# A fused attention, MoE and top-2 MoE kernel: GpSimd drains inside the expert loop, and the overflow count loaded earlier

## The chip, the cores and the metric

The kernel runs as one program on one core of a Trainium2 chip. Five engines work side by side and meet only at semaphores: TensorE (PE in the rows; its weight loads are PEld), VectorE (DVE), ScalarE (ACT), GpSimd (POOL) and SyncE (SP). Each has a sequencer that takes its instructions in order; what the sequencer itself executes (waits, branches, register loads, drains) has a q behind the engine's name in the rows, as POOLq. The metric is device time in microseconds (us), the median of several runs.

## The reference, cut to what matters

The inputs are 4 batches of 576 tokens (2304 in all) with 512 features, 8 heads, 8 experts with 1024 hidden units.

```
x   = window attention over q, k, v                  # each token sees 64 positions
x   = relu(x @ w_in)**2 @ w_out                      # first MoE block: one dense MLP, 512 -> 2048 -> 512
lg  = x @ w_gate + log1p(exp(x @ w_noise)) * noise   # 8 noisy logits a token
top2, weights = two largest logits and their softmax
for e in range(8):                                   # second MoE
    for k in range(2):
        rows = top2[:, k] == e
        out[rows] += weight * (relu(x[rows] @ w1[e]) @ w2[e])
```

## The kernel before, in words

The program has four stretches. Attention for 2304 tokens and the dense MLP are interleaved, in six groups of 384 tokens. Gating runs along with it and writes a table: for each of 8 experts 624 slots (CAP, five tiles of up to 128), and in each slot a token and its weight. The second MoE then goes through the experts in nine passes (the loop at L709): passes 0 and 1 are the two halves of expert 0, passes 2 to 8 are experts 1 to 7. Behind the last pass stands a loop for tokens that found no slot (L782). Its trip count comes from the data, and here it is zero: the engines branch past it.

GpSimd has three kinds of work in the second MoE:

- `prep` gathers the rows of the next pass's tokens from DRAM into SBUF, five indirect DMAs of 128 rows a pass (L546, tiles `gx`). TensorE transposes them.
- `split` (L147) makes two parts of each expert weight tile: ScalarE writes the first, and GpSimd the second as a difference (L149, tile `w`), 16 for each expert. They are made for the expert that comes next, so TensorE needs them a pass later.
- `finish` (L587) gathers what earlier experts added to the output rows (`gy`, L546), VectorE computes `y` (L594), and the sums are scattered back (L552). The gathers must wait until the scatters of the expert before have landed, since they read the same tensor.

A scheduler of the framework orders the instructions of each engine: an instruction is placed when the data that it needs should be there. Instructions stay in the order of the text only where a dependence or a pin says so.

The number of overflow tiles is computed on VectorE with 14 small operations (L769 to L777). The scheduler puts them right behind the last gating, early in the second MoE. `values_load` (L780) then has every engine's sequencer load that number from SBUF into a register, with one instruction that the rows call TENSOR_LOAD. SyncE's stands early; those of the other four stand behind their last work, just ahead of the branch of the loop.

When the loop is skipped, GpSimd sets forward the semaphores that the loop's own indirect DMAs would have set (INC_SWDGE_SEM, L782), all engines go through a row of waits (L782), and the program ends (L872): each engine drains, that is, its sequencer waits until its engine has nothing left, and they meet at a barrier; GpSimd clears semaphores, and they meet again.

Of the kernel before, what the change touches and what calls it, by code (L numbers as in the profile page):

```python
# [8 lines left out]
F32 = mybir.dt.float32  # L9
F32R = mybir.dt.float32r  # L10
BF = mybir.dt.bfloat16
I32 = mybir.dt.int32
U32 = mybir.dt.uint32
AF = mybir.ActivationFunctionType
OP = mybir.AluOpType
# [25 lines left out]
def moe_kernel(ctx, tc, q, k, v, w_in, w_out, wg, wn, noise, w1, w2, out):  # L41
    nc = tc.nc
    B, H, S, D = q.shape
    N, DM = out.shape
    E, _, F2 = w1.shape
# [13 lines left out]
    CAP = 624  # L59
# [2 lines left out]
    FAR = 65536.0  # L62
    NEG = -1e30

# [1 line left out]
    consts = ctx.enter_context(tc.tile_pool(name="consts", bufs=1))  # L66
    hw = ctx.enter_context(tc.tile_pool(name="hw", bufs=2))
    xtp = ctx.enter_context(tc.tile_pool(name="xtp", bufs=2))
# [13 lines left out]
    def ps(tag):  # L82
        return psum.tile([128, 512], F32, name=tag, tag=tag, bufs={"o": 3, "h": 2, "att": 3}[tag])

# [1 line left out]
    warm = consts.tile([128, 128], BF, name="warm")  # L86
    nc.vector.memset(warm, 0.0)
    ident = consts.tile([128, 128], F32, name="ident")
# [27 lines left out]
    base = consts.tile([128, E], F32, name="base")  # L116
# [26 lines left out]
        nc.vector.tensor_copy(noi.rearrange("p t e -> p e t"),  # L143
                              pn[:, :N // 128 * E].rearrange("p (e t) -> p e t", e=E))

# [1 line left out]
    def split(dst, src):  # L147
        nc.scalar.activation(dst[:, 0], src, AF.Copy)  # L148
        nc.gpsimd.tensor_sub(dst[:, 1], src, dst[:, 0].bitcast(F32))  # L149
# [41 lines left out]
        for x in worder[len(wres):n]:  # L191
            wres[divmod(x, 2)] = moe1_half(*divmod(x, 2))

# [1 line left out]
    late = {}  # L195

    def att_loads(b, s, h0, nh, pool):
# [122 lines left out]
                    load_v(g * UG + i + 2)  # L320
                yield

# [1 line left out]
    L1out, outs, x2s = {}, {}, {}  # L324

    def products(p, n, w, x, cs=range(NCC)):
# [48 lines left out]
                nc.sync.dma_start(x2d[TG * g + 128 * t:TG * g + 128 * t + 128, :], x2)  # L375
                x2s[g].append(x2)

# [1 line left out]
    GAT = {}  # L379

    def gating(g):
# [125 lines left out]
    nc.gpsimd.iota(tok, pattern=[[128, N // 128], [0, 2]], base=1, channel_multiplier=1,  # L507
                   allow_small_or_imprecise_dtypes=True)

# [1 line left out]
    slot = {}  # L511

    def index_tables(lo, hi):
        n = hi - lo
        code = table[:, lo:hi, 0]
        V = nc.vector
        f = consts.tile([128, 2, n], F32, name=f"ixf{lo}")
        ix = consts.tile([128, n], I32, name=f"ix{lo}")
        w = consts.tile([128, n], F32, name=f"wt{lo}")
        V.tensor_add(w, table[:, lo:hi, 1], table[:, lo:hi, 2])  # L520
        # a slot that nobody took points beyond the last row, each to another one
        V.tensor_scalar(f[:, 0], code, 0.0, None, op0=OP.is_equal)
        V.tensor_scalar(f[:, 1], f[:, 0], FAR, pidx, op0=OP.mult, op1=OP.add)
        V.tensor_mul(f[:, 1], f[:, 1], f[:, 0])
        V.scalar_tensor_tensor(f[:, 1], f[:, 1], -1.0, code, op0=OP.add, op1=OP.add)
        V.tensor_copy(ix, f[:, 1])
        for j in range(n):
            slot[lo + j] = (ix[:, j:j + 1], w[:, j:j + 1])
# [16 lines left out]
    def gather(dst, src, i):  # L545
        nc.gpsimd.indirect_dma_start(  # L546
            out=dst, out_offset=None, in_=src[:, :],
            in_offset=bass.IndirectOffsetOnAxis(ap=slot[i][0][:dst.shape[0]], axis=0),
            bounds_check=N - 1, oob_is_err=False)

    def scatter(src, i):
        return nc.gpsimd.indirect_dma_start(  # L552
            out=out[:, :], out_offset=bass.IndirectOffsetOnAxis(ap=slot[i][0][:src.shape[0]], axis=0),
            in_=src, in_offset=None, bounds_check=N - 1, oob_is_err=False)
# [18 lines left out]
    def m2_L1(e, f, n, xT):  # L573
        if n <= 512:
            parts = ((0, n),)
        else:
            parts = ((0, n // 2), (n // 2, n // 2))
        h = M2["h"].tile([128, 2, n], F32R, name="h")
        for a, m in parts:
            ph = ps("h")  # L580
            products(ph, m, w2s[e, f][0], xT[:, :, :, a:a + m])
            nc.scalar.activation(h[:, 0, a:a + m], ph[:, :m], AF.Relu)  # L582
            nc.vector.scalar_tensor_tensor(h[:, 1, a:a + m], ph[:, :m], 0.0, h[:, 0, a:a + m].bitcast(F32),  # L583
                                           op0=OP.max, op1=OP.subtract)
        return h

    def finish(e, tiles, o):  # L587
        ys, sc = [], []
        for j, i in enumerate(tiles):
            if e > 0:  # L590
                m = min(128, CAP - 128 * j)
                y = hp2.tile([128, DM], F32, name="y", bufs=CT)[:m]
                gather(gy[j][:m], out, i)
                nc.vector.scalar_tensor_tensor(y, o[j][:m], slot[i][1][:m], gy[j][:m], op0=OP.mult, op1=OP.add)  # L594
            else:
                y = hw.tile([128, DM], F32, name="x2", bufs=3)
                nc.scalar.activation(y, o[j], AF.Copy, scale=slot[i][1])
            ys.append(y)
        for j, i in enumerate(tiles):
            st = scatter(ys[j], i)  # L600
            for x in sc:
                tc.declare_no_dep(st.ins, x.ins, reason="an expert's slots hold different rows")
            sc.append(st)

# [1 line left out]
    fill = []  # L606
    left = [0]

# [4 lines left out]
    def filler(n):  # L613
        while n > 0 and fill:
            gen = fill.pop(0)
            try:
                next(gen)
                n -= 1
                left[0] -= 1
                fill.append(gen)  # L620
            except StopIteration:
                pass
# [13 lines left out]
    for h0 in range(0, H, HL):  # L636
        for s in range(TG // SB):
            ld, parts = att_loads(0, s, h0, HL, att0)
# [23 lines left out]
    for g in range(NG):  # L662
# [42 lines left out]
    passes = [(0, list(range(TT))), (0, list(range(TT, CT)))] + [  # L705
        (e, list(range(CT * e, CT * e + CT))) for e in range(1, E)]
    xcur = xA
    gy = []
    for n, (e, tiles) in enumerate(passes):  # L709
        T = 128 * len(tiles) if e == 0 else CAP  # L710
        if n == 1:
            GAT["pool"].release()
            ringb.release()
            hp2 = tc.alloc_tile_pool(name="hp2", bufs=2)
            M2["stg"].release()
            stg3 = tc.alloc_tile_pool(name="stg3", bufs=4)
            M2["x"] = xp2 = tc.alloc_tile_pool(name="xp2", bufs=2, side="right")
        if n == 2:
            M2["h"] = hp2
        if n == 1:  # L720
            M2["stg"] = stg3
        pending = []
        o = None
        hprev = None
        for f in range(NF2 + 1):
            if f < NF2:
                h = m2_L1(e, f, T, xcur)
            filler(1)
            if f == (P0F if n == 0 else PNF) and n == 0:
                drain()  # L730
                index_tables(TT, NS)
            pending += [(hprev, w2s[e, f - 1][1])] if f else []
            if pending and not (n + 1 == len(passes) and f == NF2 - 1):
                if o is None:
                    o = [ps("o" if j < 3 else "att") for j in range(len(tiles))]
                accumulate(o, pending, f == 1, f == NF2)
                pending = []
                filler(1)
            hprev = h
            # next expert's weights  # L740
            if n >= 1 and f < NF2 and e + 1 < E:
                w2s[e + 1, f] = stage2(e + 1, f)
            if f == (P0F if n == 0 else PNF) and n + 1 < len(passes):
                nt = passes[n + 1][1]
                if n == 0:
                    xnext = xtp.tile([128, 2, NCC, 256], F32R, name="xT")
                else:
                    xnext = M2["x"].tile([128, 2, NCC, 128 * CT], F32R, name="x2T2")
                add_fill(prep(nt, xnext), len(nt))
        drain()  # L750
        if e > 0 and not gy:
            for j in range(CT):
                t = hp2.tile([128, DM], F32, name=f"gy{j}", bufs=1)
                nc.vector.memset(t, 0.0)
                gy.append(t)
        finish(e, tiles, o)
        if n + 1 < len(passes):
            xcur = xnext
# [1 line left out]
    V = nc.vector  # L760
    M2["x"].release()
    gxp.release()
    stg3.release()
    hp2.release()
    ovp = tc.alloc_tile_pool(name="ovp", bufs=1)
    nt = consts.tile([128, E], F32, name="nt")
    ni = consts.tile([128, E], I32, name="ni")
    te = consts.tile([128, E + 1], F32, name="te")
    V.tensor_scalar(nt, base, float(CAP), 0.0, op0=OP.subtract, op1=OP.max)  # L769
    V.tensor_scalar(nt, nt, 127.0, None, op0=OP.add)  # L770
    V.tensor_copy(ni, nt)
    V.tensor_scalar(ni, ni, 7, None, op0=OP.logical_shift_right)
    V.tensor_copy(nt, ni)
    V.memset(te[:, :1], 0.0)
    for e in range(E):
        V.tensor_add(te[:, e + 1:e + 2], te[:, e:e + 1], nt[:, e:e + 1])
    V.tensor_copy(ni[:, :1], te[:, E:])  # L777
    it = consts.tile([128, 1], F32, name="it")
    V.memset(it, 0.0)
    n_more = nc.values_load(ni[0:1, 0:1], min_val=0, max_val=2 * N // 128)  # L780
    NT2 = 2 * N // 128
    with tc.For_i(0, n_more):  # L782
        ee, pp, ww = (info[:, c].rearrange("p t j -> p (t j)") for c in range(3))
        tt = tok.rearrange("p t j -> p (t j)")
        oh = ovp.tile([128, NT2, E], F32, name="oh2")
# [90 lines left out]
```

## Time and profile before

| | us |
|---|---|
| median of 3 runs | 1067.27 (1066.27 to 1068.43) |
| span of the profiled execution, first to last instruction | 1071.7 |
| TensorE busy in it | 1020.3 |
| GpSimd busy in it | 410.5 |

The profiled execution has its span as its own time; it lies 4.4 us above the median of the runs that were not profiled. In the rows below, "busy" counts an engine's own work and leaves out what its sequencer does. A view by source line lists the sequencer's instructions too, and those are what the end of this kernel consists of.

### The profile page before, as it was taken

How to read it: one execution, taken by the hardware profiler on the slowest of the kernel's cores; microseconds unless marked ns; L12 is line 12 of the kernel's file. 1: busy time of each engine (PE TensorE's matmuls, PEld its weight loads, DVE VectorE, ACT ScalarE, POOL GpSimd, SP SyncE). 2: the span in 40 equal slices, each digit the busy share in tenths (PEclk: the TensorE clock that was granted, in tenths of full speed). 3: DMA queues.
4: the chain of work that ended last, by engine and by line, in shares of the span. 5: the costliest groups of instructions: out<-in, count | busy, mean ns of one | idle time of the engine just before them, and what ended most of it. 6: DMA issues, size and time to landing. Idle time of an engine off the chain costs nothing. (4 is left out here: it accounts for less than half of the span.)

```text
span 1071.7 us, 16784 instructions
## 1 busy us (share of the span) xinstructions
PE 1020.3 (95%) x6120; PEld 902.0 (84%) x6120; DVE 509.4 (48%) x1195; ACT 418.0 (39%) x1037; POOL 410.5 (38%) x405
## 2 busy tenths in 40 slices
PE   8877899999999999999899989999999999999994
PEld 6655788888888888888789879889988989998883
DVE  7999967437635744744854612131313122222311
ACT  4655555335434444543433235333323333323210
POOL 3565632001100210200450077666665657573501
PEclk9999899999999999999999989999999999999997
DMA  9655546112112112102320245443444445351201
GB/s 197 176 169 154 152 131 211 39 36 71 35 35 76 34 29 75 39 20 60 109 70 33 77 131 180 149 136 123 144 143 124 145 124 165 103 157 57 91 1 46
DMA packets 148736, 108.33 MB, mean 101 GB/s; under 512 B 85753, under 2 KB 126713, under 8 KB 148651
## 3 DMA queue, kind: packets, MB, share of 16 engines
q1 hardware_dynamic: 139451, 80.09, 26.2%
q0 software_dynamic: 9200, 27.14, 8.1%
q8 instruction: 50, 0.82, 0.3%
q14 instruction: 35, 0.29, 0.1%
HBM read 89.27 MB, written 20.48 MB: 102 GB/s over the span
## 5 line engine op out<-in xcount | busy, mean ns | idle before, releaser
L346 PE MATMUL o<-w,h 128*128 128x512 f32 x1488 | 393.0, 402 | 20.7 <-DVE h L359 12.5
L346 PEld LDWEIGHTS o<-w,h 128*128 128x128 f32 x1488 | 270.9, 189 | 78.7 <-DVE h L359 15.8
L329 PE MATMUL h<-xT,w 128*128 128x384 f32 (+1 forms) x1344 | 263.8, 344 | 3.2 <-DVE xT L287 1.9
L329 PEld LDWEIGHTS h<-xT,w 128*128 128x128 f32 x1344 | 231.5, 192 | 8.7 <-POOL w L149 2.4
L149 POOL TENSOR_TENSOR w<-st,w 128x512 fp32r<-128x512 f32 x128 | 165.3, 1299 | 102.6 <-ACT w L148 82.8
L329 PE MATMUL h<-x2T,w 128*128 128x312 f32 x1344 | 201.4, 306 | 0.0
L329 PEld LDWEIGHTS h<-x2T,w 128*128 128x128 f32 x1344 | 195.8, 188 | 3.6
L583 DVE SCALAR_TENSOR_TENSOR h<-h 128x312 fp32r<-128x312 f32 (+2 forms) x128 | 61.9, 484 | 278.9 <-ACT h L582 263.1
L148 ACT ACTIVATE w<-st 128x512 fp32r<-128x512 f32 x128 | 80.7, 631 | 193.3 <-PE att L346 119.7
L268 POOL TENSOR_TENSOR P<-P,stat 128x384 f32<-128x384 f32 x48 | 41.8, 872 | 219.2 <-DVE stat L267 103.7
L356 ACT ACTIVATE r<-h 128x384 f32<-128x384 f32 x96 | 46.7, 487 | 142.2 <-PE h L329 124.2
L582 ACT ACTIVATE h<-h 128x312 fp32r<-128x312 f32 (+2 forms) x128 | 54.5, 425 | 120.1 <-PE h L329 115.0
L346 PE MATMUL att<-w,h 128*128 128x512 f32 (+1 forms) x336 | 94.3, 393 | 0.0
L358 DVE TENSOR_TENSOR r<-r 128x384 f32<-128x384 f32 x80 | 53.9, 673 | 69.8 <-ACT h L357 68.5
L346 PEld LDWEIGHTS att<-w,h 128*128 128x128 f32 (+1 forms) x336 | 61.0, 181 | 15.4
L359 DVE TENSOR_TENSOR h<-r,h 128x384 fp32r<-128x384 f32 x96 | 60.6, 631 | 4.9 <-POOL r L358 2.2
L546 POOL DMA_INDIRECT gx<-x2d,ix x40 | 40.9, 1023 | 50.5 <-PE att L564 41.3
L552 POOL DMA_INDIRECT out_dram<-y,ix x35 | 34.5, 985 | 45.3 <-DVE y L594 38.4
L357 ACT ACTIVATE h<-r 128x384 fp32r<-128x384 f32 x96 | 50.2, 523 | 1.5
L265 ACT ACTIVATE P<-P,stat 128x128 f32<-128x128 f32 x96 | 37.6, 392 | 28.0 <-DVE stat L263 23.6
L149 POOL TENSOR_TENSOR w<-x,w 128x512 fp32r<-128x512 f32 x24 | 35.4, 1480 | 27.0 <-ACT w L148 26.8
L546 POOL DMA_INDIRECT gy<-out_dram,ix x35 | 35.6, 1017 | 26.1 <-issue 12.9
(208 smaller groups left out, 988.4 us busy)
## 6 DMA issues: line engine op xcount, KB each, us to landing
st<-in_moe_w_dram SPq DMA_DIRECT2D x128, 256.0 KB, 3.4
st<-in_moe_w_in_dram SPq DMA_DIRECT2D x16, 512.0 KB, 4.9
st<-in_moe_w_out_dram SPq DMA_DIRECT2D x16, 512.0 KB, 4.5
vn<-in_v_dram SPq DMA_DIRECT2D x110, 64.0 KB, 2.1
x2d<-x SPq DMA_DIRECT2D x18, 256.0 KB, 3.4
out_dram<-x SPq DMA_DIRECT2D x1, 4608.0 KB
qn<-in_q_dram SPq DMA_DIRECT2D x40, 96.0 KB, 3.2
kn<-in_k_dram SPq DMA_DIRECT2D x28, 128.0 KB, 2.8
```

What stands on the lines that cost most here:

```text
L148: nc.scalar.activation(dst[:, 0], src, AF.Copy)
L149: nc.gpsimd.tensor_sub(dst[:, 1], src, dst[:, 0].bitcast(F32))
L268: nc.gpsimd.tensor_mul(P, P, st[:, :, 3:4].to_broadcast([128, 3, 128]))
L329: nc.tensor.matmul(p[:, :n], w[:, wi, 128 * c:128 * c + 128], x[:, xi, c], start=(c == 0 and i == 0), stop=(c == NCC - 1 and i == 2))
L346: nc.tensor.matmul(o[t][:hs.shape[1]], hs, w[:, wi], start=(first and i == 0 and hi == 0 and wi == 0), stop=(last and i == len(steps) - 1 ...
L356: nc.scalar.activation(r, ph[:, :TG], AF.Relu)
L357: nc.scalar.activation(h[:, 0], r, AF.Square)
L358: (nc.vector if g else nc.gpsimd).tensor_mul(r, r, r)
L359: nc.vector.tensor_sub(h[:, 1], r, h[:, 0].bitcast(F32))
L546: nc.gpsimd.indirect_dma_start(out=dst, out_offset=None, in_=src[:, :], in_offset=bass.IndirectOffsetOnAxis(ap=slot[i][0][:dst.shape[0]], ...
L582: nc.scalar.activation(h[:, 0, a:a + m], ph[:, :m], AF.Relu)
L583: nc.vector.scalar_tensor_tensor(h[:, 1, a:a + m], ph[:, :m], 0.0, h[:, 0, a:a + m].bitcast(F32), op0=OP.max, op1=OP.subtract)
```

## The change

Two things change; some comment lines go as well, which moves line numbers (the loop was L782 and is L795, the end was L872 and is L885).

First, `nc.gpsimd.drain()` is called in the pass loop: behind `finish` in passes 0 to 7, and ahead of `finish` in pass 8. A drain has no operands. `keep_in_program_order` ties it to the GpSimd instruction that was written just before it: it can't be placed ahead of that one. Nothing ties later instructions to it.

Second, the 14 operations of the count and `values_load` move into a function, `count_more`, which is called in pass 2, behind `finish` and ahead of that pass's drain.

```
@@ pass loop @@
                 gy.append(t)
+        if n + 1 == len(passes):
+            tc.keep_in_program_order(nc.gpsimd.drain())
         finish(e, tiles, o)
+        if n == 2:
+            count_more()
         if n + 1 < len(passes):
+            tc.keep_in_program_order(nc.gpsimd.drain())
             xcur = xnext
...
+    def count_more():
+        nt = consts.tile([128, E], F32, name="nt")
...
+        V.tensor_copy(ni[:, :1], te[:, E:])
+        more['te'] = te
+        more['n'] = nc.values_load(ni[0:1, 0:1], min_val=0, max_val=2 * N // 128)
...
-    n_more = nc.values_load(ni[0:1, 0:1], min_val=0, max_val=2 * N // 128)
     NT2 = 2 * N // 128
-    with tc.For_i(0, n_more):
+    te = more['te']
+    with tc.For_i(0, more['n']):
```

In the built program only GpSimd's stream differs; on the other four engines every instruction, the register loads among them, stands where it stood. The rows below leave drains and bare waits out, so the text says where the drains are.

GpSimd at the start of the second MoE, before. The L493 and L496 lines are the last gating's; the `gx` gathers are those for pass 1.

```order
L493 TENSOR_TENSOR x2T<-Bo,tok 128x6x40
L496 TENSOR_TENSOR x2T<-Bo,wh 128x6x40
L496 TENSOR_TENSOR x2T<-Bo,wl 128x6x40
L546 DMA gx_5500<-x2d,ix_6507 128x512
L546 DMA gx_5502<-x2d,ix_6507 128x512
```

The same place now:

```order
L493 TENSOR_TENSOR x2T<-Bo,tok 128x6x40
L496 TENSOR_TENSOR x2T<-Bo,wh 128x6x40
L496 TENSOR_TENSOR x2T<-Bo,wl 128x6x40
L623 TENSOR_LOAD ni
L546 DMA gx_5500<-x2d,ix_6507 128x512
L546 DMA gx_5502<-x2d,ix_6507 128x512
```

The register load has come here from the end of the program, and with it the drain of pass 2, which is tied to it: that drain stands between the load and the first gather, ahead of the scatters of pass 2 and not behind them.

GpSimd behind the scatters of pass 2 (expert 1), before:

```order
L552 DMA out_dram<-y,ix_6507 2304x512
L149 TENSOR_TENSOR w<-st_7494,w 128x512
L546 DMA gy_7413<-out_dram,ix_6507 128x512
L546 DMA gy_7415<-out_dram,ix_6507 128x512
L546 DMA gy_7417<-out_dram,ix_6507 128x512
```

The same place now:

```order
L552 DMA out_dram<-y,ix_6507 2304x512
L546 DMA gy_7415<-out_dram,ix_6507 128x512
L149 TENSOR_TENSOR w<-st_7529,w 128x512
L546 DMA gy_7417<-out_dram,ix_6507 128x512
L546 DMA gy_7419<-out_dram,ix_6507 128x512
```

One weight split has moved behind the first gather; no drain stands here.

GpSimd at the end, before:

```order
L546 DMA gy_7419<-out_dram,ix_6507 128x512
L546 DMA gy_7421<-out_dram,ix_6507 112x512
L552 DMA out_dram<-y,ix_6507 2304x512 x5
L780 TENSOR_LOAD ni
L782 COMPARE_AND_BRANCH
L782 ISA
```

The same place now:

```order
L546 DMA gy_7421<-out_dram,ix_6507 128x512
L546 DMA gy_7423<-out_dram,ix_6507 112x512
L552 DMA out_dram<-y,ix_6507 2304x512 x5
L795 COMPARE_AND_BRANCH
L795 ISA
```

The load is gone from here. Two drains, that of pass 7 and that of pass 8, stand next to each other ahead of the five `gy` gathers of pass 8, of which the last two are shown.

All in all GpSimd issues 115 indirect DMAs ahead of the end in both programs. In the new one the drains cut them into runs of 3, 10, 7, 30, 15, 15, 15, 10, 0 and, between the last added drain and the end, 10.

## Rows read from the trace of the kernel before

**Rows 1.** The page: span, busy time by engine, and the chain that ended last.
```profile
span 1071.7 us, 16784 instructions
...
PE 1020.3 (95%) x6120; PEld 902.0 (84%) x6120; DVE 509.4 (48%) x1195; ACT 418.0 (39%) x1037; POOL 410.5 (38%) x405
...
POOLq L780 0%; POOL out_dram L552 0%
```
**Rows 2.** Windows: stretch, length, each engine's busy us, clock, DMA share, GB/s.
```profile
640.00:690.00 50.00, 50.00 (x306) 45.69 (x305) 10.89 (x21) 21.66 (x43) 38.35 (x33) 1.00 0.54 172
...
747.00:804.00 57.00, 57.00 (x331) 51.36 (x330) 14.27 (x26) 18.57 (x37) 35.80 (x31) 1.00 0.43 135
...
1058.00:1060.00 2.00, 0.00 (x0) 0.00 (x0) 0.00 (x0) 0.00 (x0) 0.00 (x0) 0.95 0.30 90
1060.00:1062.00 2.00, 0.00 (x0) 0.00 (x0) 0.00 (x0) 0.00 (x0) 0.00 (x0) 0.50 0.03 8
1062.00:1071.00 9.00, 0.00 (x0) 0.00 (x0) 0.00 (x0) 0.00 (x0) 0.00 (x0) 0.50 0.00 0
```
**Rows 3.** Line L872, the end: count, duration min/median/max in ns, first and last start.
```profile
L872 SPq DRAIN  x3: 7/7/13, 1060.9 to 1071.1; - x3
L872 POOLq DRAIN  x3: 51/98/9454, 1061.4 to 1071.4; - x3
...
L872 DVEq DRAIN  x2: 10/14/17, 1061.3 to 1071.1; - x2
```
**Rows 4.** Line L861, the program's start.
```profile
L861 POOLq INC_SWDGE_SEM  x1: 27/27/27, 0.2 to 0.2; - x1
...
L861 POOLq DRAIN  x1: 181/181/181, 0.4 to 0.4; - x1
```
**Rows 5.** Indirect DMAs by line, from the page and the view of the tile out_dram.
```profile
L546 POOL DMA_INDIRECT gx<-x2d,ix x40 | 40.9, 1023 | 50.5 <-PE att L564 41.3
...
L546 POOL DMA_INDIRECT gy<-out_dram,ix x35: 992/1005/1072, 667.4 to 1013.9; - x35
L552 POOL DMA_INDIRECT out_dram<-y,ix x35: 957/974/1034, 712.1 to 1056.7; - x35
L552 POOL DMA_INDIRECT out_dram<-x,ix x5: 979/1016/1029, 626.1 to 662.5; - x5
```
**Rows 6.** Lines L780 and L782: GpSimd's register load and semaphore increment.
```profile
L780 POOLq TENSOR_LOAD <-ni x1: 712/712/712, 1056.5 to 1056.5; - x1
...
L782 POOLq INC_SWDGE_SEM  x1: 2494/2494/2494, 1057.5 to 1057.5; - x1
```
**Rows 7.** Timeline, start of the second MoE: start, us, engine, operation, [idle before <-releaser].
```profile
612.40 0.60 POOL L496 TENSOR_TENSOR x2T<-Bo,wl 128x240 fp32r<-128x240 f32 x1
613.43 0.15 DVE L777 CAST ni<-te 128x1 int32<-128x1 f32 x1
616.92 1.04 POOL L546 DMA_INDIRECT gx<-x2d,ix  x1 [3.92 <-DVE ix L526]
622.07 0.63 PE L564 MATMUL att<-ident,gx 128*128 128x128 f32 x4 [0.69 <-DMA gx<-x2d,ix]
628.73 0.98 POOL L552 DMA_INDIRECT out_dram<-x,ix  x1 [0.30 <-issue]
632.16 2.51 POOL L149 TENSOR_TENSOR w<-st,w 128x512 fp32r<-128x512 f32 x2 [2.46 <-ACT w L148]
```
**Rows 8.** Timeline of GpSimd behind the scatters of passes 2 and 3.
```profile
719.41 1.32 POOL L149 TENSOR_TENSOR w<-st,w 128x512 fp32r<-128x512 f32 x1
723.50 1.07 POOL L546 DMA_INDIRECT gy<-out_dram,ix  x1 [2.78 <-issue]
...
775.90 0.96 POOL L552 DMA_INDIRECT out_dram<-y,ix  x1 [0.17 <-issue]
776.87 1.31 POOL L149 TENSOR_TENSOR w<-st,w 128x512 fp32r<-128x512 f32 x1
780.77 1.07 POOL L546 DMA_INDIRECT gy<-out_dram,ix  x1 [2.60 <-issue]
```
**Rows 9.** Timeline of GpSimd in the last pass.
```profile
1005.57 0.96 POOL L552 DMA_INDIRECT out_dram<-y,ix  x1 [0.17 <-issue]
1008.60 1.07 POOL L546 DMA_INDIRECT gy<-out_dram,ix  x1 [2.07 <-DMA out_dram<-y,ix]
...
1051.16 1.03 POOL L552 DMA_INDIRECT out_dram<-y,ix  x1 [36.27 <-DVE y L594]
...
1056.72 0.96 POOL L552 DMA_INDIRECT out_dram<-y,ix  x1 [0.41 <-DVEq L782]
```

More of the change, by code (lines that the diff above doesn't have):

```diff
@@ L603, in finish @@
             sc.append(st)
+    more = {}
+    def count_more():
+        nt = consts.tile([128, E], F32, name="nt")
+        ni = consts.tile([128, E], I32, name="ni")
+        te = consts.tile([128, E + 1], F32, name="te")
+        V = nc.vector
+        V.tensor_scalar(nt, base, float(CAP), 0.0, op0=OP.subtract, op1=OP.max)
+        V.tensor_scalar(nt, nt, 127.0, None, op0=OP.add)
+        V.tensor_copy(ni, nt)
+        V.tensor_scalar(ni, ni, 7, None, op0=OP.logical_shift_right)
+        V.tensor_copy(nt, ni)
+        V.memset(te[:, :1], 0.0)
+        for e in range(E):
+            V.tensor_add(te[:, e + 1:e + 2], te[:, e:e + 1], nt[:, e:e + 1])
+        V.tensor_copy(ni[:, :1], te[:, E:])
+        more['te'] = te
+        more['n'] = nc.values_load(ni[0:1, 0:1], min_val=0, max_val=2 * N // 128)
     fill = []
@@ L765, in moe_kernel @@
     ovp = tc.alloc_tile_pool(name="ovp", bufs=1)
[L766 to L777, printed above, removed]
     it = consts.tile([128, 1], F32, name="it")
     V.memset(it, 0.0)
-    n_more = nc.values_load(ni[0:1, 0:1], min_val=0, max_val=2 * N // 128)
     NT2 = 2 * N // 128
-    with tc.For_i(0, n_more):
+    te = more['te']
+    with tc.For_i(0, more['n']):
         ee, pp, ww = (info[:, c].rearrange("p t j -> p (t j)") for c in range(3))
```

## The prediction

> **What bounds the kernel now.** I read the page first: TensorE is busy 1020.3 of 1071.7 us [rows 1]. The windows say the same of the experts: in the 57 us of one pass TensorE is busy for all 57.00, and GpSimd for 35.80 [rows 2]. So in the body TensorE sets the pace, and GpSimd has 57 − 35.8 = 21.2 us to spare a pass. The chain of waits is no help: it ends in the last scatter and the register load at 0% each [rows 1], because what follows isn't an engine's work. What follows is 14 us: the last scatter starts at 1056.72 and is issued by 1057.68 [rows 9], the span ends at 1071.7. From 1062 to 1071 no engine does anything and the DMA share is 0.00 [rows 2]. The view of the last line names what fills it: three drains on GpSimd, of which one lasts 9454 ns, from 1061.4, so to 1070.9 [rows 3]. That is 0.9% of the span with nothing beside it, and the change is about this drain.
>
> **What the long drain waits for.** Not for data: the DMA share is 0.30 in the two microseconds ahead of 1060, 0.03 in the next two and then nothing [rows 2]. Not a fixed price of the instruction: the other two drains of that line take 51 and 98 ns [rows 3], and the one at the program's start, with four small fills before it, 181 ns [rows 4]. So it grows with something that GpSimd did since the last drain. What sets this stretch apart is 40 + 35 + 35 + 5 = 115 indirect DMAs [rows 5]; the two short drains behind it have none before them.
>
> The Trainium skill ("VectorE: DVE Perf Modes", section "The DRAIN you can't avoid") says that drains of a kernel's frame take some 12 ns each, the same on all five engines. SyncE's and VectorE's agree, at 7 to 17 ns [rows 3]; GpSimd's 9454 ns doesn't, and the measurement decides. By that rule a drain would be worth nothing, at the end or anywhere, and the time would stay.
>
> **The change part by part.**
>
> *The drain at the end.* Before, it has 115 indirect DMAs behind it; afterwards the last added drain stands ahead of the `gy` gathers of pass 8, so 5 gathers and 5 scatters are left. If the price goes by their number it is 9.454 / 115 = 0.082 us each, and 10 cost 0.82 us. That saves 8.63 us. From both sides: at most 9.454 − 0.181 = 9.27 us go, when what is left costs no more than the drain at the start [rows 3, 4]; at the least nothing goes, when the number doesn't count. I take 8.63, since the short drains stand by the side of "few behind it, little to do".
>
> *The added drains.* The other 105 DMAs are settled at the added drains, 105 × 0.082 = 8.6 us of GpSimd in all, and each is to be hidden where it stands.
> - The drain of pass 2, tied to the register load, runs early. The number is ready at 613.43 + 0.15 = 613.6, the load takes 0.71 [rows 6, 7], so the drain starts at about 614.4 with 3 DMAs behind it: 0.25 us. The next gather can't start before 616.92, since it waits for VectorE's indices [rows 7]. Slack 2.5 us, cost nothing. This is the one sharp place: TensorE waits for these gathers already (0.69 us at 622.07 [rows 7]), so what the drain takes beyond 2.5 us is lost.
> - The drain behind pass 0 has 10 DMAs, 0.82 us from 629.7; the next split starts at 632.16, held by ScalarE [rows 7]. Hidden. Pass 1, with 7, takes 0.57 us.
> - Behind pass 3 there are 30 DMAs: 2.5 us from 776.9, and a split of 1.31 us then ends at 780.7, while the next gather starts at 780.77, when the scatters have landed [rows 8]. It just fits. Passes 4 to 6 have 15, so 1.23 us, at the same place.
> - If a drain also sat out the landing of the scatters before it, it would end at about 780.8 instead (that gather shows when they have landed), and what follows on GpSimd would come 1.3 us later, one split; the 21.2 us to spare hide it, since splits serve the next pass and `gy` is used at the pass's end.
> - The two ahead of pass 8's gathers have 10 and none, 0.82 us from 1006.5, and the gathers start at 1008.60 behind the landing of the scatters [rows 9]. Hidden; and the scatters come 36 us later.
>
> *The split that moves behind a gather in pass 2* starts at about 724.6 instead of 719.4 [rows 8], 5 us late in a pass with 21.2 us to spare. Nothing.
>
> *The register load* leaves GpSimd's end: 0.71 us [rows 6]. But it ran beside the last scatter, which ends at 1057.68 [rows 9], and the increment behind it ran from 1057.5 to 1060.0 [rows 6], as long as the scatters' data were moving [rows 2]. Between 0 and 0.71 us; I take 0, because the scatter, not the load, is what the increment has just behind it. The other engines' loads stay where they are.
>
> *Sum.* 1071.7 − 8.6 = 1063.1 us for the profiled span. The runs that weren't profiled have a median of 1067.27, 4.4 less than the span; I carry that distance over, 1067.27 − 8.6 = 1058.7 us. Should all 4.4 us lie in the drain, it lasts 5.0 us in those runs, and 5.0 × 105 / 115 = 4.6 go: 1062.7 us. With 9.27 + 0.71 = 10.0 gone it is 1057.3. So the forecast's own range is 1057.3 to 1062.7.
>
> **The rivals.**
>
> *The drain's length belongs to the end itself* (say to the increment that the skipped loop needs, which stands ahead of it at 1057.5 and takes 2.49 us [rows 6]). Then the added drains cost their 0.1 us each, the end keeps its 9.45, and the time is 1067.3. For it: increment and drain follow each other. Against it: by 1060.0 the increment is over [rows 6], and at the program's start the same two instructions follow each other and that drain takes 181 ns [rows 4].
>
> *The price is capped.* If only the last pass or two count, 15 to 30 DMAs carry the whole 9.27 us, and the 10 that are left keep 10/15 to 10/30 of it: 3.1 to 6.2 us go, 1061.1 to 1064.2, middle 1062.6. Nothing in the trace speaks against it; nothing shows a cap.
>
> *Slower: a drain takes its 9.45 us whenever any indirect DMA stands before it.* Then the end keeps 9.45, and the drain at 614.4 lasts until 623.9 with the gathers behind it, 7.0 us after 616.92. TensorE, which already waits there, loses these 7.0: 1074.3. It decides as soon as a drain with few DMAs behind it takes over 2.5 us. In the later passes even 9.45 us fit in the 21.2. For it: no row has a drain with few DMAs behind it. Against it: only that the price would not depend on the amount at all.
>
> *The price is paid once,* by whichever drain first has indirect DMAs before it. Then the end gains 8.6 and the drain at 614.4 loses the 7.0: 1065.7. The Trainium skill ("GPSIMD Engine Reference", section "2.1 Instruction dispatch") has such a mechanism: the first call into freshly loaded GpSimd code pays about 6 us that no instruction shows. No run here shows it.
>
> **How the numbers follow.** The forecast, 0.60: 1058.7. Capped price, 0.12: 1062.6. Belongs to the end, 0.14: 1067.3. Paid once, 0.06: 1065.7. Full price each time, 0.08: 1074.3. A run of this kernel scatters by 2 us around the median, so 0.2%, 2.1 us, is what can be told from no change. Faster by more than that is below 1065.1: 0.60 + 0.12 = 0.72. Within it: 0.14 + 0.06 = 0.20. Slower: 0.08. The range starts at 1057.0 and must reach past the unchanged time, since 0.20 lie near it: 1057.0 to 1068.2, which leaves out the slower case alone, with the scatter at both ends.
>
> **What would show it.** In the profile of the changed kernel the first GpSimd drain of the last line should take 0.7 to 1.0 us and the span end about 1063. Drains on the new lines should take some 0.25, 0.8, 0.6, 2.5, 1.2 (three times) and 0.8 us, in step with the DMAs behind them; equal lengths point to a fixed price, one long and the rest short to a price paid once. TensorE's wait for `gx` near 622 should stay below 1 us. A drain at the end that still takes over 3 us makes the forecast wrong, and a TensorE wait of several microseconds near 622 turns its sign.

## The result, and the profile after

The changed kernel takes 1057.12 us (median of 4 runs, 1056.36 to 1058.12); the kernel before, run beside it, 1066.77 us (4 runs, 1065.03 to 1068.43). The ratio is 0.9907, 95% interval 0.9895 to 0.9920: 9.65 us less, by the interval 8.5 to 11.2. The forecast was 8.6 less and 1058.7. The long drain shrank as forecast; the gain is about 1 us larger, and a part of that is a term that the prediction put at nothing. By the times alone, 8.6 and 9.65 can't be told apart, since 8.6 lies in the interval; the traces show the term.

The line of the kernel's end answers to [rows 3]: count, duration min/median/max in ns, first and last start.

```profile
L885 POOLq EVENT_SEMAPHORE  x4: 17/17/17, 1054.3 to 1054.9; - x4
L885 SPq DRAIN  x3: 7/7/13, 1053.1 to 1054.5; - x3
L885 POOLq DRAIN  x3: 51/98/862, 1053.4 to 1054.8; - x3
```

The drain that took 9454 ns takes 862; its two neighbours, 51 and 98 ns, are as they were. The forecast was 0.82 us left and 8.63 saved; it is 0.86 left and 8.59 saved.

The line of the skipped loop, where the increment stands and the engines then wait for all that is still under way, answers to [rows 6]. First after, then before (its exit waits, not shown until now):

```profile
L795 SPq EVENT_SEMAPHORE  x21: 17/28/2526, 966.6 to 1052.9; - x21
...
L795 POOLq EVENT_SEMAPHORE  x13: 42/43/2247, 1049.3 to 1053.1; - x13
...
L795 POOLq INC_SWDGE_SEM  x1: 404/404/404, 1049.4 to 1049.4; - x1
```

```profile
L782 SPq EVENT_SEMAPHORE  x21: 17/27/28, 973.8 to 1060.7; - x21
...
L782 POOLq EVENT_SEMAPHORE  x13: 42/43/43, 1057.4 to 1061.2; - x13
```

Two things are to be seen. The increment shrank from 2494 to 404 ns, which the prediction had not priced. And the wait behind it changed owner: before, none of these waits lasts over 43 ns, because by the end of the increment (1060.0) all scatters had landed; after, one of them lasts 2247 ns on GpSimd and 2526 on SyncE: now the last scatter's landing (the arrival of its data) comes last.

The windows of the end answer to [rows 2]: stretch, length, busy us of PE, PEld, DVE, ACT, POOL, granted clock, DMA share, GB/s.

```profile
640.00:1040.00 400.00, 400.00 (x2323) 361.51 (x2322) 98.96 (x177) 125.15 (x251) 233.29 (x203) 1.00 0.39 123
...
1050.00:1052.00 2.00, 0.00 (x0) 0.00 (x0) 0.00 (x0) 0.00 (x0) 0.31 (x1) 1.00 0.39 123
1052.00:1054.00 2.00, 0.00 (x0) 0.00 (x0) 0.00 (x0) 0.00 (x0) 0.00 (x0) 0.52 0.03 8
1054.00:1055.00 1.00, 0.00 (x0) 0.00 (x0) 0.00 (x0) 0.00 (x0) 0.00 (x0) 0.50 0.00 0
```

In the body TensorE is busy for all 400 of 400 us, so the added drains make it wait nowhere in them. At the end, what follows the window with a DMA share of 0.03 was 9.7 us long (1062.0 to 1071.7) [rows 2] and is 1.0 us (1054.0 to 1055.0). The last scatter starts here:

```profile
1049.35 0.96 POOL L552 DMA_INDIRECT out_dram<-y,ix  x1 [0.41 <-DVEq L795]
```

From that start to the span's end it is 1055.0 − 1049.35 = 5.65 us; before, 1071.7 − 1056.72 = 14.98 [rows 1, 9]. Of the 9.33 us between them 8.59 are the drain. The rest, about 0.7, is the stretch from the scatter's start to the drain's: 4.7 us before (1056.72 to 1061.4), 4.0 after (1049.35 to 1053.4).

The added drains (first the one ahead of the last expert, then the eight others), and one of them in GpSimd's timeline (start, us, engine, operation, [idle before <-releaser]):

```profile
L777 POOLq DRAIN  x1: 53/53/53, 1001.4 to 1001.4; - x1
```

```profile
L782 POOLq DRAIN  x8: 305/8202/13997, 613.7 to 994.4; - x8
```

```profile
612.91 0.15 DVE L621 CAST ni<-te 128x1 int32<-128x1 f32 x1
616.39 1.04 POOL L546 DMA_INDIRECT gx<-x2d,ix  x1 [3.92 <-DVE ix L526]
621.17 0.63 PE L564 MATMUL att<-ident,gx 128*128 128x128 f32 x4 [0.32 <-DMA gx<-x2d,ix]
...
768.53 0.96 POOL L552 DMA_INDIRECT out_dram<-y,ix  x1 [0.17 <-issue]
774.16 1.28 POOL L149 TENSOR_TENSOR w<-st,w 128x512 fp32r<-128x512 f32 x1 [4.67 <-PE att L346]
775.59 1.07 POOL L546 DMA_INDIRECT gy<-out_dram,ix  x1 [0.15 <-issue]
```

The first drain, at the one sharp place, takes 0.305 us (0.25 forecast) and ends well before the gather at 616.39, which starts as far behind VectorE's count (3.48 us) as before (3.49 [rows 7]). TensorE's wait there is 0.32 us, against 0.69 in the first profile of before and 0.30 in its second (shown further down), so nothing was lost there and nothing gained. The other records are long, 8.2 us in the middle, because a drain's record begins while GpSimd still works off what was queued ahead of it. What a drain holds up is read from the gap: behind pass 3 the last scatter ends at 769.49 and the next split starts at 774.16, a gap of 4.67 us, where the forecast had 2.5 of drain or 3.9 with the landing. The `gy` gather follows it at 775.59; before, it stood 4.87 us behind the scatter's start [rows 8], now 7.06. Nobody waits for that: the window above is full.

### The profile page after: what moved, and what is told of

The parts are those of the page before. It is cut to its first block, busy times and chain, and to the rows that moved or that the text cites. A ratio compares the mean times of both kernels' runs of the same rounds, so it can differ in the third digit from the quotient of the medians.

```text
span 1055.0 us, 16793 instructions
## 1 busy us (share of the span) xinstructions
PE 1017.3 (96%) x6120; PEld 899.5 (85%) x6120; DVE 509.1 (48%) x1195; ACT 417.8 (40%) x1037; POOL 409.6 (39%) x405
## 4 chain that ended last, share of the span: by engine, by line
PE 78%; DVE 10%; issue 6%; ACT 2%; POOL 1%; DMA 1%; POOLq 0%; SPq 0%; ACTq 0%; DVEq 0%
PE h L329 34%; PE o L346 27%; PE att L346 6%; PE att L255 2%; PE att L283 2%; DVE x L161 2%; PE att L564 2%; DVE x L162 1%; PE att L272 1%; DVE h L359 1%; DVE x L160 1%; PE att L396 1%; ACT P L265 1%; DVE r L358 1%; POOL out_dram L552 1%
```

## The experiments

**Two parts apart: the drains without the early load.** The theories for the 0.7 us of the end that the drain doesn't explain: the register load is worth it after all (prediction: 0), or something else at the end shrank with the drain.

```
-        if n == 2:
-            count_more()
...
+    count_more()
     it = consts.tile([128, 1], F32, name="it")
```

> All added drains stay, and the register load goes back to the end of GpSimd's program, behind the last scatters. Theory A (the drain's price goes by the indirect DMAs since the last one, and the load at the end is worth 0.7 us): the first end drain stays at 0.86 us, the increment starts 0.7 us later than in the changed kernel, and the time is 1057.1 + 0.7 = 1057.8 us, 0.9914 of before. Theory B (the load is worth nothing, as the prediction had it, and all of the gain is the drain): 1057.1 us, 0.9907, with the same drain. Theory C (moving the load is what shortens the end drain): end drain 9.4 us, 1066.8 us.

`count_more()` now stands behind the loop over the passes. With the load gone from its early place, the drain of pass 2 stands behind that pass's scatters, so the first drain is that of pass 0.

1057.51 us (4 runs), ratio 0.9910 [0.9893, 0.9928]. Times can't tell 1057.1 from 1057.8 here, but the trace can: the load is back at the end, and the end is as short as in the changed kernel.

```profile
L623 POOLq TENSOR_LOAD <-ni x1: 707/707/707, 1048.0 to 1048.0; - x1
```

```profile
L794 POOLq EVENT_SEMAPHORE  x13: 43/43/1419, 1049.0 to 1052.0; - x13
...
L794 POOLq INC_SWDGE_SEM  x1: 399/399/399, 1049.1 to 1049.1; - x1
```

```profile
L884 POOLq DRAIN  x3: 51/98/862, 1052.2 to 1053.6; - x3
```

```profile
1048.27 0.96 POOL L552 DMA_INDIRECT out_dram<-y,ix  x1 [0.41 <-DVEq L794]
```

The increment starts 0.8 us behind the last scatter's start (1048.27 to 1049.1), where with the load early it starts with it (1049.35 and 1049.4). Yet from the scatter's start to the drain it is 4.0 us (1048.27 to 1052.24), no longer than with the load early: a wait of 1.4 us for the landing absorbs the delay. So theory A's part on the load falls: beside the drains, moving it buys nothing. What shrank with the load in its old place is the increment: 399 ns.

**One drain instead of nine, ahead of the last expert's gathers; and one behind them.** These two kernels have none of the other added drains; the code shown here and further down leaves out some of the lines that take drains away.

```
         if n + 1 < len(passes):
-            tc.keep_in_program_order(nc.gpsimd.drain())
             xcur = xnext
```

> A single added drain, ahead of the last expert's gathers, with 105 indirect DMAs behind it; the load is at the end. Theory A: that drain needs about 0.04 + 105 x 0.082 = 8.6 us beyond the landing of the scatters ahead of it, hidden in GpSimd's spare time; the end drain is 0.86 us, and the time that of the kernel with all drains and the load at the end, 1057.8 us. Rival (a drain settles only a limited amount, or the drains behind each pass are all needed): the end drain stays well over 1 us, and the time is above 1060 us.

```
                 gather(gy[j][:m], out, i)
+                if e == E - 1 and j + 1 == len(tiles):
+                    tc.keep_in_program_order(nc.gpsimd.drain())
```

> A single added drain, behind the last expert's five gathers and ahead of its five scatters; the load is at the end. Theory A: 5 indirect DMAs are left, the end drain takes 0.04 + 5 x 0.082 = 0.45 us, 0.41 us less than with ten, and the time is 0.4 us below that of the single drain ahead of the gathers, about 1057.4 us. Rival (0.86 us is the floor of an end drain that has anything before it): end drain 0.86 us, 1057.8 us.

Without the other drains nothing holds the load early, so in both it stands at the end. 1057.16 us (ratio 0.9901 [0.9885, 0.9918]) and 1056.62 us (0.9897 [0.9881, 0.9914]). The first's single drain and the gap that it makes, with 105 indirect DMAs issued before it:

```profile
L777 POOLq DRAIN  x1: 13412/13412/13412, 995.2 to 995.2; - x1
```

```profile
999.04 0.96 POOL L552 DMA_INDIRECT out_dram<-y,ix  x1 [0.17 <-issue]
1009.97 1.07 POOL L546 DMA_INDIRECT gy<-out_dram,ix  x1 [9.96 <-issue]
```

```profile
L884 POOLq DRAIN  x3: 51/98/868, 1054.7 to 1056.1; - x3
```

It ends at 995.2 + 13.4 = 1008.6, 8.6 us behind the last scatter's end at 1000.0: the price forecast for 105, with no landing on top (the scatters land within those 8.6 us). All of it is hidden, and the end drain is what nine drains had left. The second kernel's end drain, with five scatters left:

```profile
L884 POOLq DRAIN  x3: 51/98/460, 1053.5 to 1054.5; - x3
```

460 ns: no floor at 0.86. The nine drains are worth no more than one; the 0.4 us between the two kernels' drains are seen in the traces, but their times' intervals overlap.

**The same single late drain, with the load early.**

```
...
         if n + 1 < len(passes):
+            if n == 2:
+                tc.keep_in_program_order(nc.gpsimd.drain())
```

> The drain that ties the register load to an early place, and one drain behind the last expert's gathers; no others. Theory A: end drain 0.45 us and the load's 0.7 us gone as well, so 0.4 us below the changed kernel: 1056.7 us, 0.9903 of before; 0.7 us below the kernel with the same late drain and the load at the end. Theory B (the load is worth nothing): the same time as that kernel, 1057.4 us or 0.9910.

1057.48 us, 0.9901 [0.9882, 0.9920]: not faster than with the load at the end. This is theory B's side, though the runs of one kernel lie 2.8 us apart here (1055.62 to 1058.38), too far to tell 0.7 by time. The end drain is again short:

```profile
L886 POOLq DRAIN  x3: 51/98/455, 1054.9 to 1055.9; - x3
```

**One drain in the middle: is the price capped, or paid once?**

```
         if n + 1 < len(passes):
+            if n == 3:
+                tc.keep_in_program_order(nc.gpsimd.drain())
```

> A single added drain, behind the scatters of pass 3 (the fourth pass); 50 indirect DMAs stand before it and 65 behind it. Theory A (price by number, without a cap): the end drain takes 0.04 + 65 x 0.082 = 5.4 us, and the time is about 4.1 us below before, 1062.7 us. Rival, a capped price (15 to 30 DMAs carry the whole): end drain 9.4 us, time of before. Rival, paid once by the first drain that has indirect DMAs before it: end drain below 0.2 us.

```profile
L884 POOLq DRAIN  x3: 51/98/5360, 1054.7 to 1060.6; - x3
```

```profile
L794 POOLq EVENT_SEMAPHORE  x13: 42/43/332, 1051.4 to 1054.5; - x13
...
L794 POOLq INC_SWDGE_SEM  x1: 1493/1493/1493, 1051.5 to 1051.5; - x1
```

5.36 us for 65 DMAs, theory A's 5.4; both rivals fall. The time is 1062.33 us against 1066.87, ratio 0.9953 [0.9936, 0.9971], 4.5 us less. The increment is in between as well, 1.49 us. The added drain itself and the work around it:

```profile
L781 POOLq DRAIN  x1: 9900/9900/9900, 766.2 to 766.2; - x1
```

```profile
769.89 0.96 POOL L552 DMA_INDIRECT out_dram<-y,ix  x1 [0.17 <-issue]
776.25 1.30 POOL L149 TENSOR_TENSOR w<-st,w 128x512 fp32r<-128x512 f32 x1 [5.40 <-ACT w L148]
```

With 50 before it, it ends at 766.2 + 9.9 = 776.1, some 5.2 us behind the last scatter's end, where the bare price is 4.1.

**What the price goes by.** Ten further gathers behind the last added drain, short in one kernel and full in the other:

```
+        if n + 1 == len(passes):
+            for k in range(10):
+                gather(gx[k % CT][:16], out, tiles[k % CT])
```

The other kernel has `[:112]` in place of `[:16]`.

> The changed kernel with ten further gathers of 16 rows each behind its last added drain (into the gx tiles, which nothing reads any more), so that 20 indirect DMAs of 1280 - 80 + 160 rows are left for the end. Price by number of DMAs: end drain 0.04 + 20 x 0.082 = 1.68 us. Price by rows moved: 0.86 x (1 + 160/1200) = 0.97 us. Price by elapsed time or by GpSimd's other work: 0.86 us.

> The same with ten further gathers of 112 rows each. Price by number of DMAs: end drain 1.68 us. Price by rows moved: 0.86 x (1 + 1120/1200) = 1.66 us, so that only the kernel with short gathers tells these two apart. Price by elapsed time or by GpSimd's other work: 0.86 us.

The end drain of the first (the second's row reads the same, word for word), and the ten gathers of the one and of the other:

```profile
L888 POOLq DRAIN  x3: 51/98/1679, 1053.6 to 1055.8; - x3
```

```profile
L546 POOL DMA_INDIRECT gx<-out_dram,ix x10: 886/890/935, 1002.6 to 1013.4; - x10
```

```profile
L546 POOL DMA_INDIRECT gx<-out_dram,ix x10: 987/992/1027, 1002.2 to 1013.9; - x10
```

1679 ns both times: what counts is the number of DMAs, not rows, time or other work. One run each: 1058.10 and 1058.07 us.

**The cover taken away.** A single drain between the last expert's first and second scatter:

```
             st = scatter(ys[j], i)
+            if e == E - 1 and j == 0:
+                tc.keep_in_program_order(nc.gpsimd.drain())
```

> A single added drain, between the first and the second scatter of the last expert, where nothing on GpSimd is left to hide it: 111 indirect DMAs before it, 4 behind. Theory A (a drain holds up GpSimd's queue for 0.04 + 0.082 us per indirect DMA since the last one, and cover alone makes it free): the drain takes 9.1 us from the first scatter's end, the last scatter starts 8.6 to 9.0 us later than with the drain behind the gathers, the end drain takes 0.37 us, and the time is 1056.6 + 8.7 = 1065.3 us, 0.998 of before: the change's gain is lost. Rival (an added drain is cheap wherever it stands, because the long price belongs to the end alone or because GpSimd goes on beside it): 1056.5 us.

```profile
1044.80 1.02 POOL L552 DMA_INDIRECT out_dram<-y,ix  x1 [36.30 <-DVE y L594]
1055.78 0.99 POOL L552 DMA_INDIRECT out_dram<-y,ix  x1 [9.97 <-issue]
...
1059.64 0.96 POOL L552 DMA_INDIRECT out_dram<-y,ix  x1 [0.30 <-issue]
```

```profile
L884 POOLq DRAIN  x3: 51/98/378, 1063.6 to 1064.5; - x3
```

The end drain has fallen to 0.38 us, but GpSimd stands still for 9.97 us between two scatters, and the time is 1066.56 us (10 runs) against 1066.61 (13), ratio 0.9998 [0.9989, 1.0008]. The whole gain is gone: an added drain takes no work away, it moves it, and only the place pays. My 1065.3 was 1.3 too low; the last scatter started 14.84 us after the first, 9.3 more than in the kernel with the drain behind the gathers (5.56), where 8.7 was expected. That explains 0.6 of the 1.3; the rest is open. The increment, with four indirect DMAs since the last drain, is the shortest of all kernels, and its record starts ahead of the last scatter's (1059.64):

```profile
L794 POOLq INC_SWDGE_SEM  x1: 273/273/273, 1058.3 to 1058.3; - x1
```

**The kernel before once more.** The profile read for the prediction was 4.4 us longer than the runs.

> The kernel before once more, for a second profile. If the profile read for the prediction was longer than its runs because of the TensorE wait of 4.0 us near 628 and the 6.8 us at the lower clock behind it: this one has neither, its end drain is again 9.4 to 9.5 us, and its span is about 1065 us. If the runs have a shorter drain than that profile: a span near 1065 us with a drain of about 5 us.

Its own time is 1067.11 us, span 1065.3. The end drain, and the windows near 628, first of this one and then of the first profile:

```profile
L872 POOLq DRAIN  x3: 51/98/9454, 1055.0 to 1065.0; - x3
```

```profile
610.00:640.00 30.00, 29.70 (x180) 26.73 (x179) 9.80 (x29) 12.70 (x25) 21.58 (x21) 1.00 0.41 123
```

```profile
610.00:640.00 30.00, 25.35 (x136) 22.46 (x135) 8.52 (x23) 8.77 (x17) 17.78 (x18) 0.89 0.32 98
```

```profile
631.61 2.93 PE L346 MATMUL o<-w,h 128*128 128x512 f32 x6 [3.97 <-ACT h L582]
```

The median, shortest and longest drain of that line are the same to the nanosecond. The first profile had a disturbance of its own in the body: TensorE did 4.35 us less in that window. It stood idle for 3.97 us up to 631.6, behind ScalarE's `h`, and the granted clock is 0.89 over the window, so for a part of it the lower of its two levels, 1.2 GHz. A span here is 1.8 to 2.1 us below its run's own time, so the first profile's own time was some 1073.6 us, an estimate.

This second profile is undisturbed, so it can be set against that of the changed kernel part by part. Its lines, then one of the changed kernel's that was not shown yet:

```profile
613.87 0.15 DVE L777 CAST ni<-te 128x1 int32<-128x1 f32 x1
617.37 1.04 POOL L546 DMA_INDIRECT gx<-x2d,ix  x1 [3.94 <-DVE ix L526]
622.14 0.63 PE L564 MATMUL att<-ident,gx 128*128 128x128 f32 x4 [0.30 <-DMA gx<-x2d,ix]
...
1044.78 1.02 POOL L552 DMA_INDIRECT out_dram<-y,ix  x1 [36.09 <-DVE y L594]
...
1050.34 0.96 POOL L552 DMA_INDIRECT out_dram<-y,ix  x1 [0.41 <-DVEq L782]
```

```profile
1043.79 1.02 POOL L552 DMA_INDIRECT out_dram<-y,ix  x1 [35.02 <-DVE y L594]
```

From the first `gx` gather to the first of the last five scatters it is 427.41 us before and 427.40 after: the added drains cost the body nothing. The five scatters take 5.56 us from first to last start in both. The spans differ by 1065.3 − 1055.0 = 10.3 us: 8.59 in the drain, 0.7 on the way to it (1050.34 to 1055.0 before, 4.0 us after), and 1.0 ahead of VectorE's count (613.87 and 612.91), where the two programs don't differ. That 1.0 us is spread between executions: in the ten profiles other than the disturbed one this count stands between 611.75 and 614.30, whatever the kernel.

## Where the prediction was right, and the step that failed

The price of the end drain and of the increment, by the indirect DMAs since the last drain, from the profiles of all kernels:

```
indirect DMAs   end drain, ns   INC_SWDGE_SEM, ns
4                    378              273
5                455, 460        293, 298
10               862 to 868      393 to 404
20                  1679              594
65                  5360             1493
115                 9454        2493, 2494
per DMA   (9454-378)/111 = 81.8   (2494-273)/111 = 20.0
```

The rows of 4 and 5 are scatters alone, fifteen of the 20 are gathers, and all lie on one line: both kinds cost the same.

- *The end drain.* Right: 0.86 us for ten (0.82 forecast), and a straight line from 4 to 115. The choice of 8.63 out of a range from 0 to 9.27 us holds because the price goes by their number. That was an assumption: the trace of before had drains with 115 and with none, and nothing between them; the experiments bear it out.
- *The added drains.* Their place was judged rightly, their size too low where scatters had just been issued: 4.67 us of gap behind pass 3 instead of 2.5. In the kernels with nine drains they end 2.2 to 4.6 us behind the last scatter and not at the bare price; the branch "a drain also sits out the landing" is nearer. With 105 before it the bare price, 8.6 us, covers the landing; with 50 it ends 5.2 us behind the last scatter, where the bare price is 4.1, and how price and landing add up is not settled. Spare time hid both, as said.
- *The sharp place at 614.* Right: 0.305 us, no TensorE time lost.
- *The register load.* Taken as 0, and beside the drains it is 0: with the load back at the end, the way from the last scatter to the drain is just as short. The reason given was wrong: the increment doesn't stand behind the scatter, it starts with it when the load is away (1049.4 and 1049.35), and where the last scatter was held up it starts ahead of it (1058.3 and 1059.64). The load is worth nothing because the landing comes last.
- *The step that failed: the sum, which had one term for the indirect DMAs left for the end where there are two.* The prediction looked at the increment [rows 6], but took its 2.49 us to last as long as the scatters' data moved, and used it otherwise only in a rival for the drain's length; what the change would do to it was put at nothing. It goes by the same number of DMAs, 20 ns each, so it fell by 2.09 us too. Not all of that is gained: before, load and increment held up the exit, until 1060.0 (0.8 + 2.5 us behind the scatter's start, and 1.4 more to the drain, 4.7 in all); now the landing does. By the two profiles the end gains 0.7 us so. Over the nine profiles with at most 65 DMAs left, the way from the last scatter to the drain is 4.0 to 4.6 us, against 4.7 in both profiles of before: the term is worth 0.1 to 0.7, depending on when the scatters land. 8.6 + 0.1 to 0.7 = 8.7 to 9.3 us, and 9.65 [8.5, 11.2] was measured. The increment was not tried apart from the drain, since both go by the same number; nor was the early load without any drain, because without one the load stays at the end.
- *The carried distance.* Carrying 4.4 us from the span to the runs was right in effect: the drain is equal in both profiles of before. Its reason was missing: the first profile was disturbed in the body. Of the 1.58 us between 1058.7 and 1057.12, 0.5 are the median of before, which a fourth run moved from 1067.27 to 1066.77; over its 31 runs beside all these kernels it is 1066.87. What is left of 9.65, 0.35 to 0.95 us, lies within the spread of the runs. The profiles show a spread of 2.5 us ahead of VectorE's count, where the programs don't differ; whether it makes this remainder of the medians stays open.
- *The rivals.* "Belongs to the end" and "paid once" fall with 5.36 us for 65 DMAs, as does the cap. "Full price each time" falls with 0.305 us behind three DMAs; it would also be the only one to be slower. Its core, that what a drain holds up matters where cover is missing, is true and cost all the gain when the cover was taken away.
- The Trainium skill ("VectorE: DVE Perf Modes", section "The DRAIN you can't avoid") has some 12 ns for a frame's drain on every engine: VectorE's and SyncE's agree (7 to 17 ns), GpSimd's takes 51 to 98 ns with no indirect DMA since the last drain, and 378 to 9454 with 4 to 115.

The best version by its median has one drain, behind the last expert's gathers: 1056.62 us, 0.9897 of before. It isn't told apart from the changed kernel (0.9907) by these runs.

## What to carry to other kernels

Where a kernel issues many indirect DMAs from GpSimd, look at the drains of its last line: their cost is a bill for all DMAs since the last drain, and one drain placed earlier, where GpSimd has time to spare and nothing behind it is urgent, pays it under cover. Count the DMAs that come after it, and set it as late as cover allows. All DMAs that GpSimd issues here are indirect ones, so no run shows whether others add to the bill. And when a wait at the end shrinks, look at every instruction of the same stretch whose length may go by the same count, and at which wait is then last.

## What was not expected of the hardware

- The semaphore increment behind the skipped loop grows by 20 ns for each indirect DMA since the last drain, just as the drain does by 82 ns. The two lines differ at zero: carried down from 4, the drain's meets 51 ns, which is what a drain with none takes; the increment's meets 193 ns, while the one at the program's start takes 27 [rows 4]. What the difference is made of is not shown.
- A gather of 16 rows costs a later drain as much as one of 112, and issuing it takes 890 ns of GpSimd against 992: both are paid by the instruction more than by the row.
- A drain's record in the profile can be 8 us long where it holds up the engine for 2 to 5, since it begins before the engine has worked off its queue; the gap in the engine's timeline is what it costs.
